# A chunked attention with a rational feed-forward layer on one core: loads sent in pieces behind the streamed sums, plain products in the last two steps

## The chip, the core and the metric

The kernel runs on one core of a Trainium2 chip. The metric is device time in microseconds (us) of one execution. Engines are named as in the profile: PE is TensorE (its weight loads are PEld), DVE is VectorE, ACT is ScalarE, POOL is GpSimd, SP is SyncE, which here only issues DMAs. All numbers are float32; the matmuls take operands split into a high part that TensorE holds exactly and a low rest, and add three products for each (high by high, high by low, low by high).

## What is computed

```
scores = scale * q_c @ k_c.T                  # chunks of 64 tokens, 8 heads of 64, batch 8, 576 tokens
attn = exp(scores - max) / (sum + 1e-9)
x = attn @ v_c                                # 4608 tokens x 512
h = x @ w_in                                  # 512 x 2048
P = a[0] + a[1] * h + a[2] * h**2 + a[3] * h**3
Q = 1.0 + abs(b[0]) * abs(h) + abs(b[1]) * h**2
out = (P / (Q + 1e-6)) @ w_out                # 2048 x 512
```

## The kernel before

**Blocks and steps.** The 4608 tokens are 18 blocks of 256 (`n`, 0 to 17), the 2048 columns of `h` four stages of 512 (`s`). A step `g` is one stage of one block; from block 2 on, g = 4n + s, so there are 72 steps and the last two are 70 and 71. A step is: `ff1`, the product with `w_in` (48 matmuls of 128x256 in two calls, F and Fb, at L347) into the PSUM tile `ph`; a chain of twelve or so elementwise operations on ACT and DVE that ends with `g` at L486 in the tile `C`; and the product with `w_out`. That last product runs two steps behind: on PE the order is F of step g, then the `w_out` product of step g - 2, then F of step g + 1.

**Two forms of the last product.** Up to block 5 it is plain (`ff2`, L423, 48 matmuls of 256 columns, operands `ghi` and `glo`). From block 6 (`FAST`) it is a seven-product scheme that multiplies sums of quarters of `C` by sums of quarters of `w_out` and takes 42 matmuls: `fast_raw` (calls Zr, Zr2; operand `graw`) and `fast_sum` (calls Zs, Zl; operands `shi`, `slo`). The quarters' sums of `C` are made on POOL (L513, L518, L523, L537, and L505 for `graw`). The sums of `w_out` are made once (`sums_of`, on POOL and ACT, tiles `tt` and `hh`, in steps 12 to 21), sent to DRAM, and **streamed** back for each step into four slots of the tile `wo`: `fetch` at L579, 2 MB a step. Slot 0 is fetched when Zr2 of the step before has read it, the low part (h = 1) of slots 1 to 3 after its Zs, the high part (h = 0) after its Zl. So from the end of Zl until Zs of the next step, with F, Zr and Zr2 between, the last 768 KB must land.

**Order of the work.** The order is written out by hand: `START` up to step 11, then `STEADY`, a table of calls for one block that is run for each block in turn; each engine takes its own calls in this order, and so does SP's queue of DMAs. In one block of `STEADY` there are also the parts of the attention of the next blocks: S (scores, PE, 64 matmuls of 64x64), M, U, E, rs, N (softmax on DVE and ACT), T (transposes on PE), K (`at`, a copy on ACT at L303), A (values, PE), X, Y. S comes in the middle of a `w_out` product, after Zr of stage 1; right behind it `next_scores` (L754) issues the loads of the next block's query and key (512 KB each). A comes in the `w_out` product of stage 0; right behind it `load_v` (L130) issues 512 KB of value. `fast_out` adds the seven products up on ACT and DVE (calls P1, o1 to o4; L624 to L636) and issues four DMAs of the output (L640). Making the sums hangs on the call lS, which subtracts `glo` on POOL in the plain steps (L540): after each lS of steps 12 to 21 six pieces of `sums_of` are taken from the list `making`.

**Tiles.** One pool tag, `raw`, has three buffers of 8 KB a partition: during the sums they hold `tt`, `hh` and `qk`, later `graw0`, `graw1` and `qk`. `co` holds the coefficients.

## Time and profile before

| | |
|---|---|
| Median of 3 runs | 937.63 us (936.0 to 939.81) |
| The profiled execution, its own time | 939.04 us |
| Its span, first to last instruction | 937.3 us |
| PE, PEld busy | 93%, 91% |
| DVE, ACT, POOL busy | 80%, 60%, 54% |
| DMA, mean over the span | 176 GB/s |
| Granted TensorE clock, mean | 0.978 of full speed |

The times and rows of the trace come from one profiled execution, whose span leaves out 1.7 us around it. A busy share is a mean over stages; the question for each stage is which engine the others wait for. In the timeline a row's bracket gives the idle time of its engine just before it and what ended it.

### The profile page before, as it was taken

The numbers are of one execution on the slowest core, as the hardware profiler recorded it, in microseconds if no ns is written. First come the engines' busy times: TensorE is split into PE (matmuls) and PEld (weight loads), VectorE is DVE, ScalarE is ACT, GpSimd is POOL, SyncE is SP. The second block draws the span as 40 slices with busy tenths as digits, with TensorE's granted clock in tenths as the row PEclk, the third lists the DMA queues.
The fourth block names the chain that finished last, engine by engine and source line by source line (L and its number), as shares of the span: only waits on it lengthen the run. The fifth ranks groups of instructions, "written<-read, shape, count | busy, mean of one in ns | idle before, by whom it ended". The sixth has DMA issues, their size and how long they took to land.

```text
span 937.3 us, 20950 instructions
## 1 busy us (share of the span) xinstructions
PE 870.3 (93%) x9096; PEld 848.7 (91%) x9096; DVE 749.6 (80%) x673; ACT 562.9 (60%) x602; POOL 506.2 (54%) x318
## 2 busy tenths in 40 slices
PE   2799999989989999998999999999989999999985
PEld 1789999989989999898998999998989999999985
DVE  6899999867767687887778797878878889897771
ACT  4799966464455655555465656556556565666550
POOL 0114210236668635666567666675756767676672
PEclk9799999999999999999999999999999999999997
DMA  7455422102233243767576766667667777666673
GB/s 290 159 181 172 155 80 77 38 21 66 96 135 136 70 165 100 232 212 237 180 247 204 229 212 218 221 208 232 206 195 226 226 222 224 210 210 197 206 232 112
DMA packets 119099, 164.93 MB, mean 176 GB/s; under 512 B 5856, under 2 KB 104160, under 8 KB 115936
## 3 DMA queue, kind: packets, MB, share of 16 engines
q1 hardware_dynamic: 118848, 163.34, 54.4%
q8 instruction: 71, 1.16, 0.5%
q10 hardware_dynamic: 160, 0.26, 0.1%
q14 instruction: 20, 0.16, 0.1%
HBM read 145.76 MB, written 17.83 MB: 175 GB/s over the span
## 4 chain that ended last, share of the span: by engine, by line
PE 72%; DMA 13%; ACT 6%; DVE 5%; POOL 3%; issue 1%; DVEq 0%; SPq 0%; POOLq 0%; ACTq 0%
PE ph L347 34%; PE acc L594 12%; DMA wo<-t 11%; PE acd L594 10%; PE po L423 10%; PE psx L220 2%; DMA raw<-in_w_in 2%; PE pst L299 2%; PE pss L220 2%; ACT at L303 1%; DVE sm L256 1%; POOL glo L540 1%; DMA t<-tt 1%; POOL tt L550 1%; DVE e L262 1%
## 5 line engine op out<-in xcount | busy, mean ns | idle before, releaser
L347 PE MATMUL ph<-xhi,wi_hi 128*128 128x256 f32 x1152 | 326.1, 283 | 10.8 <-ACT at L303 6.4
L347 PE MATMUL ph<-xlo,wi_hi 128*128 128x256 f32 x1152 | 322.5, 280 | 0.1
L347 PE MATMUL ph<-xhi,wi_lo 128*128 128x256 f32 x1152 | 322.3, 280 | 0.0
L347 PEld LDWEIGHTS ph<-xhi,wi_hi 128*128 128x128 f32 x1152 | 217.8, 189 | 16.2 <-ACT at L303 8.6
L347 PEld LDWEIGHTS ph<-xlo,wi_hi 128*128 128x128 f32 x1152 | 217.8, 189 | 0.5 <-DVE xlo L330 0.4
L347 PEld LDWEIGHTS ph<-xhi,wi_lo 128*128 128x128 f32 x1152 | 217.9, 189 | 0.0
L537 POOL TENSOR_TENSOR slo<-B,shi 128x1024 fp32r<-128x1024 f32 x48 | 121.7, 2536 | 85.3 <-ACT shi L529 85.3
L478 DVE SCALAR_TENSOR_TENSOR U<-U,co,ph 128x1024 f32<-128x1024 f32 x60 | 75.7, 1261 | 58.2 <-ACT ph L474 58.2
L457 DVE SCALAR_TENSOR_TENSOR U<-U,co 128x1024 f32<-128x1024 f32 x60 | 98.9, 1649 | 26.4 <-ACT U L448 26.4
L448 ACT ACTIVATE U<-ph 128x1024 f32<-128x1024 f32 x60 | 61.5, 1025 | 91.4 <-PE ph L347 91.4
L505 POOL TENSOR_TENSOR graw<-C,graw 128x768 fp32r<-128x768 f32 x48 | 98.7, 2055 | 31.0 <-ACT graw L500 24.6
L513 POOL TENSOR_TENSOR B<-C 128x512 f32<-128x512 f32 x48 | 75.1, 1564 | 70.7 <-DVE C L486 70.7
L470 ACT ACTIVATE B<-U,cst,co 128x1024 f32<-128x1024 f32 x60 | 74.8, 1246 | 54.7 <-DVE U L457 54.7
L461 DVE TENSOR_TENSOR C<-C,ph 128x1024 f32<-128x1024 f32 x60 | 72.8, 1214 | 33.6 <-ACT U L448 33.6
L423 PE MATMUL po<-wo,ghi 128*128 128x256 f32 (+2 forms) x768 | 93.5, 278 | 0.0
L453 ACT ACTIVATE C<-ph,co 128x1024 f32<-128x1024 f32 x60 | 72.2, 1204 | 31.2 <-PE ph L347 28.0
L423 PEld LDWEIGHTS po<-wo,ghi 128*128 128x128 f32 x768 | 90.6, 188 | 0.0
L594 PE MATMUL acc<-wo,graw 128*128 128x256 f32 x576 | 84.6, 281 | 1.5 <-POOL graw L505 1.5
L474 ACT ACTIVATE ph<-B,co 128x1024 f32<-128x1024 f32 x60 | 67.2, 1120 | 29.1 <-DVE C L465 26.8
L594 PE MATMUL acd<-wo,shi 128*128 128x256 f32 x384 | 64.5, 292 | 21.6 <-DMA wo<-t 19.9
L486 DVE SCALAR_TENSOR_TENSOR C<-C,co,ph 128x1024 f32<-128x1024 f32 x60 | 76.9, 1281 | 2.1
L465 DVE SCALAR_TENSOR_TENSOR C<-C,co,ph 128x1024 f32<-128x1024 f32 x60 | 76.6, 1276 | 1.1
(107 smaller groups left out, 1630.8 us busy)
## 6 DMA issues: line engine op xcount, KB each, us to landing
wo<-t SPq DMA_DIRECT2D x94, 768.0 KB, 6.5
wo<-t SPq DMA_DIRECT2D x102, 256.0 KB, 3.5
v<-in_vP SPq DMA_DIRECT2D x18, 512.0 KB, 4.8
out<-o SPq DMA_DIRECT2D x70, 128.0 KB, 2.6
raw<-in_w_in SPq DMA_DIRECT2D x8, 1024.0 KB, 4.8
raw<-in_w_out SPq DMA_DIRECT2D x8, 1024.0 KB, 4.8
qk<-in_qT SPq DMA_DIRECT2D x16, 512.0 KB, 3.6
qk<-in_kT SPq DMA_DIRECT2D x16, 512.0 KB, 5.0
```

The source lines that it names most:

```text
L347: nc.tensor.matmul(ph[:, fi, :], w[:, cc, f], x[:, cc, :], start=(k == 0), stop=(k == len(mm) - 1))
L423: nc.tensor.matmul(accs[n][i][:, cols], g[:, fi, i * 128:(i + 1) * 128], w[:, FPS * s + fi, cols], start=start, stop=stop,)
L457: nc.vector.scalar_tensor_tensor(U, U, c0, U, ALU.add, ALU.mult)
L461: nc.vector.tensor_mul(C, C, h)
L465: nc.vector.scalar_tensor_tensor(C, C, na1, h, ALU.add, ALU.mult)
L470: nc.scalar.activation(ch[key][2], ch[key][1], AF.Ln, bias=cst[:, 0:1], scale=lsc)
L478: nc.vector.scalar_tensor_tensor(V, V, kq, h, ALU.add, ALU.mult)
L486: nc.vector.scalar_tensor_tensor(C, C, na0, h, ALU.add, ALU.mult)
L505: nc.gpsimd.tensor_sub(lo, quads(ch[steps[g]][3])[:, :, 1:4, :], hi.bitcast(F32))
L513: nc.gpsimd.tensor_sub(S[:, 0:2], q[:, 0:1].to_broadcast([P, 2, 2, 128]), q[:, 1:3])
L537: nc.gpsimd.tensor_sub(lo, sbuf[g], hi.bitcast(F32))
L594: nc.tensor.matmul(acc[n][pair][:, bank, col:col + 256], stat, mov, start=start, stop=stop)
```

## The change

- **Transfers.** Query and key of the next block are no longer sent in two loads behind S but in eight of 256 columns (128 KB each), value in two of 512 columns (256 KB each), and the output's four DMAs are held back too. All go into a list, `later`; after the last fetch of a step (behind Zl) `later_loads` takes two entries from it, 512 KB in all. The output's entries are put ahead of the list.
- **Sums of `w_out`.** The list `making` is cut into groups by `None`: four operations on POOL, four on POOL, then two copies on ACT with four subtractions on POOL and the send. One group is taken at each lS, so that steps 12 to 23 make them, three to each of the four sets.
- **Last two steps.** Steps 70 and 71 take the plain form, 48 matmuls each (`tail_next`, `tail_last`), into a tile `pe` of their own, with `glo` subtracted on DVE and not on POOL. The quarter of `w_out` that the streams have overwritten is saved in DRAM when the sums are sent (`scratch["b", s]`, for stages 2 and 3) and loaded to `b12` (`tail_load`, 2 x 512 KB) at the start of block 17's turn. The seven-product sums of block 17 then end with its stage 1; `fast_out` adds them up behind lS of step 71, and two additions on DVE join them with `pe`.
- **Order.** In `STEADY` PE's own order stays as it was. On ACT E comes behind hR of stage 3, hS of stage 2 behind Ex of stage 3, hR of stage 1 ahead of Ln of stage 2, C of stage 1 ahead of U, and of stage 3 U first, then hR of stage 2, C and Ln; on DVE V of stage 3 goes ahead of M and p of stage 3 behind U; on POOL the parts of the sums of quarters change places, mostly so that `graw` of stage 2 comes before its sums.
- **Tiles.** `graw` starts 96 numbers (384 bytes) into its buffer. `co` is allocated behind the other tiles and not ahead of them, which moves every tile of the pool `p2` down by 128 bytes.

```diff
...
-    "F_0 p2_3-1 lS_2-1 Ln_3-1 Ex_3-1 Fb_0 E+1 lR_2-1 t_3-1 A2_3-1 Zr_2-1 U_0 g_3-1 C_0 Zr2_2-1 V_0 Zs_2-1 hR_3-1 "
+    "F_0 p2_3-1 s4_2-1 Ex_3-1 Fb_0 hS_2-1 t_3-1 lS_2-1 A2_3-1 Zr_2-1 U_0 g_3-1 C_0 Zr2_2-1 V_0 Zs_2-1 hR_3-1 p_0 "
...
-    co = cp.tile([P, 32], F32, tag="co", name="co")
...
+    total = NB * NST
+
     def fast(g):
-        return steps[g][0] >= FAST
+        return NST * FAST <= g < total - 2
...
         if g % 2 not in graw:
-            graw[g % 2] = p2.tile([P, 2, 2, 3, 128], F32R, tag="raw", name=f"graw{g % 2}", bufs=3)
+            t = p2.tile([P, 96 + 1536], F32R, tag="raw", name=f"graw{g % 2}", bufs=3)
+            graw[g % 2] = t[:, 96:].rearrange("p (h j q t) -> p h j q t", h=2, j=2, q=3)
         nc.scalar.copy(graw[g % 2][:, 0], quads(C)[:, :, 1:4, :])
...
-            nc.gpsimd.tensor_sub(lo, C, hi.bitcast(F32))
+            (nc.gpsimd if g < total - 2 else nc.vector).tensor_sub(lo, C, hi.bitcast(F32))
...
         T = [tt[:, i] for i in range(4)]
+        yield None
         yield lambda: whole(T[1], 0, 0)
         yield lambda: whole(T[3], 0, 1)
         yield lambda: nc.gpsimd.tensor_sub(T[1], T[3], T[1])
         yield lambda: whole(T[2], 1, 1)
+        yield None
         yield lambda: nc.gpsimd.tensor_add(T[3], T[2], T[3])
         yield lambda: nc.gpsimd.tensor_add(T[2], T[2], T[1])
         yield lambda: whole(T[0], 1, 0)
         yield lambda: nc.gpsimd.tensor_sub(T[0], T[0], T[2])
+        yield None
...
             nc.sync.dma_start(out=scratch[s][:, 0], in_=hh.bitcast(F32))
             nc.sync.dma_start(out=scratch[s][:, 1], in_=tt)
+            if s >= 2:
+                scratch["b", s] = dr.tile([P, 2, 2, 256], F32, tag=f"b{s}", name=f"b{s}")
+                rows = slice(FPS * s, FPS * s + 3, 2)
+                for h in range(2):
+                    nc.sync.dma_start(out=scratch["b", s][:, h], in_=wo.bitcast(F32)[:, h, rows, 256:512])
...
                         n, s, name, j, stat, h, s == 0 and half == 0 and j == 0 and h == 0 and name == "7",
-                        s == NST - 1 and half == 1 and j == 1,
+                        s == (1 if n == NB - 1 else NST - 1) and half == 1 and j == 1,
                     )
+
+    tail = {}
+
+    def tail_load():
+        b12 = p2.tile([P, 2, 2, 2, 256], F32R, tag="raw", name="b12", bufs=3)
+        tail["b12"] = b12
+        for k in range(2):
+            nc.sync.dma_start(out=b12.bitcast(F32)[:, k], in_=scratch["b", 2 + k])
+
+    def tail_product(g, i, fi, h, stat, start, stop):
+        _, s = steps[g]
+        for c in range(2):
+            if c == 1 and fi % 2 == 0:
+                mov = tail["b12"][:, s - 2, h, fi // 2]
+            else:
+                mov = wo[:, h, FPS * s + fi, 256 * c:256 * c + 256]
+            nc.tensor.matmul(
+                tail["pe"][:, i, 256 * c:256 * c + 256], stat[:, fi, 128 * i:128 * i + 128], mov,
+                start=start and c == 0, stop=stop and c == 1,
+            )
+
+    def tail_next(half):
+        g = total - 2
+        if half == 0:
+            tail["pe"] = bank_pair("p1", "pe")
+        stat = gbuf[steps[g]][half]
+        for fi in range(FPS):
+            for i in range(2):
+                for h in ((0, 1) if half == 0 else (0,)):
+                    tail_product(g, i, fi, h, stat, half == 0 and fi == 0 and h == 0, False)
+
+    def tail_last():
+        g = total - 1
+        hi, lo = gbuf[steps[g]]
+        for i in range(2):
+            mm = [(x, h, fi) for x, h in ((hi, 0), (hi, 1), (lo, 0)) for fi in range(FPS)]
+            for k, (x, h, fi) in enumerate(mm):
+                tail_product(g, i, fi, h, x, False, k == len(mm) - 1)
+            oe = p2.tile([P, DM], F32, tag="AB"[i], name=f"oe{i}")
+            part_ = obuf[NB - 1][:, 2 - 2 * i:4 - 2 * i].rearrange("p a b -> p (a b)")
+            nc.vector.tensor_add(oe, tail["pe"][:, i, :], part_)
+            for u, queue in ((0, nc.sync), (1, nc.scalar)):
+                queue.dma_start(out=rows_out(NB - 1)[i, u], in_=oe[64 * u:64 * u + 64, :])
...
+            if n == NB - 1:
+                return
             for c in range(2):
-                for u in range(UPB):
-                    half = o[64 * u:64 * u + 64, 2 - 2 * c:4 - 2 * c].rearrange("p a b -> p (a b)")
-                    (nc.scalar if n == NB - 1 and u else nc.sync).dma_start(out=rows_out(n)[c, u], in_=half)
+                def send(c=c):
+                    for u in range(UPB):
+                        half = o[64 * u:64 * u + 64, 2 - 2 * c:4 - 2 * c].rearrange("p a b -> p (a b)")
+                        nc.sync.dma_start(out=rows_out(n)[c, u], in_=half)
+
+                later.insert(c, send)
...
+    co = p2.tile([P, 32], F32, tag="co", name="co", bufs=1)
+    na0, na1, na2, na3, c0, kq, lsc, ebias, ib, b1m, nib = (co[:, i:i + 1] for i in range(11))
     newton_coefficients()
     tt = p2.tile([P, 4, 512], F32, tag="raw", name="tt", bufs=3)
     hh = p2.tile([P, 4, 512], F32R, tag="raw", name="hh", bufs=3)
     qk = p2.tile([P, 2, W], F32, tag="raw", name="qk", bufs=3)
...
-    making = [f for s in range(NST) for f in sums_of(s, tt, hh)]
+    making = [f for s in range(NST) for f in sums_of(s, tt, hh)][1:]
...
-                nc.sync.dma_start(out=qk[:, i, :], in_=src[n + 1])
+            for c in range(4):
+                def send(c=c):
+                    cols = slice(256 * c, 256 * c + 256)
+                    for i, src in enumerate((qT, kT)):
+                        nc.sync.dma_start(out=qk[:, i, cols], in_=src[n + 1][:, cols])
+
+                later.append(send)
...
-        load_v(n + 1)
+        if n + 1 < NB:
+            v = loaded["v", n + 1] = p2.tile([P, W], F32, tag="vt", name=f"v{n + 1}", bufs=1)
+            for c in range(2):
+                cols = slice(512 * c, 512 * c + 512)
+                later.append(lambda cols=cols: nc.sync.dma_start(out=v[:, cols], in_=vP[n + 1][:, cols]))
...
         elif op in chain:
             chain[op](g)
             if op == "lS":
-                for _ in range(6):
-                    if making:
-                        making.pop(0)()
+                while making:
+                    f = making.pop(0)
+                    if f is None:
+                        break
+                    f()
+                if g == total - 1:
+                    for k in range(5):
+                        fast_out(NB - 1, k)
+        elif g == total - 2:
+            if op in ("Zr", "Zl"):
+                tail_next(int(op == "Zl"))
+        elif g == total - 1:
+            if op == "Zl":
+                tail_last()
         elif not fast(g):
             if op == "Zr":
...
+                later_loads()
         elif op in ("Zr", "Zr2"):
             fast_raw(g, op == "Zr2")
-            if op == "Zr2" and g + 1 < total:
+            if op == "Zr2" and fast(g + 1):
                 for h in range(2):
                     fetch((s + 1) % NST, slice(0, 1), h)
         else:
             fast_sum(g, op == "Zl")
-            if g + 1 < total:
+            if fast(g + 1):
                 fetch((s + 1) % NST, slice(1, 4), 1 if op == "Zs" else 0)
+            if op == "Zl":
+                later_loads()
+
+    def later_loads():
+        for f in later[:2]:
+            f()
+        del later[:2]
 
     items = [re.fullmatch(r"(\w+?)(?:_(\d))?([+-]\d+)?", item).groups() for item in STEADY.split()]
     for b in range(FIRST // NST, NB + 1):
+        if b == NB - 1:
+            tail_load()
...
-                if n >= FAST:
+                if NB - 1 > n >= FAST:
                     fast_out(n, ("P1", "o1", "o2", "o3", "o4").index(op))
-                elif op == "P1" and n not in made["O"]:
+                elif op == "P1" and n < FAST and n not in made["O"]:
```

On SP's queue, in one block of the steady part (`t1` to `t3` and `t0` are the streamed sums of the four stages; 128x2x256 is slot 0, 128x6x256 slots 1 to 3; x2 is one for each part; `o` is the output, `v` value, `qk` query and key), there stood before:

```order
L640 DMA out_0<-o9_6278 64x512 x4
L579 DMA wo_71<-t1_2883 128x2x256 x2
L130 DMA v12_6407<-in_vP 128x1024
L579 DMA wo_71<-t1_2883 128x6x256 x2
L754 DMA qk_2003<-in_qT 128x1024
L754 DMA qk_2003<-in_kT 128x1024
L579 DMA wo_71<-t2_3179 128x2x256 x2
L579 DMA wo_71<-t2_3179 128x6x256 x2
L579 DMA wo_71<-t3_3631 128x2x256 x2
L579 DMA wo_71<-t3_3631 128x6x256 x2
```

and now:

```order
L588 DMA wo_71<-t1_3045 128x6x256 x2
L697 DMA out_0<-o9_6332 64x512 x4
L588 DMA wo_71<-t2_3471 128x2x256 x2
L588 DMA wo_71<-t2_3471 128x6x256 x2
L828 DMA v12_6458<-in_vP 128x512 x2
L588 DMA wo_71<-t3_3931 128x2x256 x2
L588 DMA wo_71<-t3_3931 128x6x256 x2
L818 DMA qk_2003<-in_qT 128x256
L818 DMA qk_2003<-in_kT 128x256
```

The loads of value and of query and key, and the output's DMAs, have moved from ahead of a step's fetches to behind the last one of them; of the four pairs of query and key pieces two go behind this step's fetches and two behind the next's.

On POOL, steps 13 to 16 (`glo` is lS, with its step's number; the rows of `tt` are pieces of `sums_of`), there stood before:

```order
L540 TENSOR_TENSOR glo13_2454<-C13_2200,ghi13_2399 128x1024
L550 TENSOR_TENSOR tt_2001<-wo_71 128x512
L560 TENSOR_TENSOR tt_2001<-tt_2001 128x512
L563 TENSOR_TENSOR tt_2001<-tt_2001,hh_2002 128x512 x2
L540 TENSOR_TENSOR glo14_2584<-C14_2338,ghi14_2535 128x1024
L563 TENSOR_TENSOR tt_2001<-tt_2001,hh_2002 128x512 x2
L550 TENSOR_TENSOR tt_2001<-wo_71 128x512 x2
L555 TENSOR_TENSOR tt_2001<-tt_2001 128x512
L550 TENSOR_TENSOR tt_2001<-wo_71 128x512
L540 TENSOR_TENSOR glo15_2741<-C15_2495,ghi15_2663 128x1024
```

and now:

```order
L541 TENSOR_TENSOR glo14_2611<-C14_2336,ghi14_2494 128x1024
L567 TENSOR_TENSOR tt_2001<-tt_2001,hh_2002 128x512 x4
L541 TENSOR_TENSOR glo15_2744<-C15_2530,ghi15_2661 128x1024
L551 TENSOR_TENSOR tt_2001<-wo_71 128x512 x2
L557 TENSOR_TENSOR tt_2001<-tt_2001 128x512
L551 TENSOR_TENSOR tt_2001<-wo_71 128x512
L541 TENSOR_TENSOR glo16_2878<-C16_2658,ghi16_2787 128x1024
```

The first operations of the second set, which write `tt` again, stood right behind the four subtractions after which `tt` is sent; now `glo15` and a step's time lie between, and no `glo` waits behind more than four operations.

On DVE, at the end of the program (`U71` and `C71` are tiles of step 71's chain, `o17` the output of block 17), there stood before:

```order
L478 SCALAR_TENSOR_TENSOR U71_10439<-U71_10439,co_76,ph17_3_10366 128x1024
L482 SCALAR_TENSOR_TENSOR ph17_3_10366<-U71_10439,ph17_3_10366 128x1024
L486 SCALAR_TENSOR_TENSOR C71_10437<-C71_10437,co_76,ph17_3_10366 128x1024
L630 TENSOR_TENSOR o17_10590<-acc17_10305,o17_10590 128x2x256
L632 TENSOR_TENSOR o17_10590<-acd17_10306,o17_10590 128x2x256
L634 TENSOR_TENSOR o17_10590<-acd17_10306,o17_10590 128x512
L636 TENSOR_TENSOR o17_10590<-acc17_10305,o17_10590 128x256
```

and now:

```order
L478 SCALAR_TENSOR_TENSOR U71_10531<-U71_10531,co_1991,ph17_3_10461 128x1024
L541 TENSOR_TENSOR glo70_10574<-C70_10412,ghi70_10533 128x1024
L482 SCALAR_TENSOR_TENSOR ph17_3_10461<-U71_10531,ph17_3_10461 128x1024
L486 SCALAR_TENSOR_TENSOR C71_10536<-C71_10536,co_1991,ph17_3_10461 128x1024
L541 TENSOR_TENSOR glo71_10629<-C71_10536,ghi71_10611 128x1024
L684 TENSOR_TENSOR o17_10631<-acc17_10395,o17_10631 128x2x256
L686 TENSOR_TENSOR o17_10631<-acd17_10396,o17_10631 128x2x256
L688 TENSOR_TENSOR o17_10631<-acd17_10396,o17_10631 128x512
L690 TENSOR_TENSOR o17_10631<-acc17_10395,o17_10631 128x256
L668 TENSOR_TENSOR oe0_10661<-pe_10577,o17_10631 128x512
L668 TENSOR_TENSOR oe1_10689<-pe_10577,o17_10631 128x512
```

The additions of block 17 have moved behind `glo71` and no longer wait for the product of step 71, the subtraction `glo70` has come into step 71's chain, and two additions (`oe0`, `oe1`) are last.

## Rows read from the trace of the kernel before

**Rows 1.** The profile's page: the busy time of each engine (share of the span, number of instructions).

```profile
PE 870.3 (93%) x9096; PEld 848.7 (91%) x9096; DVE 749.6 (80%) x673; ACT 562.9 (60%) x602; POOL 506.2 (54%) x318
```

**Rows 2.** The waits, longest first in total, for PE over the whole span: who waited for whom, us in total, times, longest us.

```profile
PE acd L594 <- DMA wo<-t: 20.5, 12, 3.7
...
PE ph L347 <- ACT at L303: 6.4, 11, 4.7
```

**Rows 3.** The timeline of PE, from the first seven-product block on: first matmuls of F of some steps (`ph<-xhi,wi_hi`), and a wait in front of Zs (`acd<-wo,shi`). Columns: start us, us, engine, line, operation, out<-in, count, and in brackets the idle time before it and what ended it.

```profile
361.65 0.29 PE L347 MATMUL ph<-xhi,wi_hi 128*128 128x256 f32 x1
...
761.61 0.28 PE L347 MATMUL ph<-xhi,wi_hi 128*128 128x256 f32 x1
...
773.49 0.36 PE L347 MATMUL ph<-xhi,wi_hi 128*128 128x256 f32 x1
...
782.60 0.70 PE L594 MATMUL acd<-wo,shi 128*128 128x256 f32 x4 [1.10 <-DMA wo<-t]
...
831.19 0.28 PE L347 MATMUL ph<-xhi,wi_hi 128*128 128x256 f32 x1
...
842.73 0.39 PE L347 MATMUL ph<-xhi,wi_hi 128*128 128x256 f32 x1 [0.18 <-ACT at L303]
...
854.73 0.28 PE L347 MATMUL ph<-xhi,wi_hi 128*128 128x256 f32 x1
...
865.34 0.28 PE L347 MATMUL ph<-xhi,wi_hi 128*128 128x256 f32 x1
```

**Rows 4.** The chain of work that ended last, in order of time (start us, us, what): the 48 matmuls of F in two steps, and two waits for a fetch, counted from the end of Zl before it.

```profile
773.36 9.11 DMA wo<-t
...
808.79 9.15 DMA wo<-t
...
821.06 5.44 PE ph L347 x48
...
865.50 5.66 PE ph L347 x48
```

**Rows 5.** Busy time of each engine in some stretches (us from the span's start; the last three columns are the granted clock, the mean busy share of the 16 DMA engines, and GB/s).

```profile
686.00:690.00 4.00, 3.55 (x20) 3.58 (x21) 3.90 (x6) 2.15 (x2) 3.92 (x4) 0.67 0.34 98
...
812.00:814.00 2.00, 2.00 (x20) 2.00 (x19) 1.93 (x3) 0.74 (x1) 1.18 (x1) 1.00 1.07 379
...
816.00:818.00 2.00, 1.84 (x70) 1.57 (x62) 1.26 (x2) 1.37 (x2) 1.84 (x3) 1.00 0.05 11
...
820.00:830.00 10.00, 10.00 (x90) 10.00 (x89) 8.59 (x7) 6.30 (x6) 5.18 (x3) 1.00 0.63 196
...
914.00:918.00 4.00, 3.62 (x17) 3.65 (x18) 0.10 (x1) 0.83 (x1) 3.68 (x3) 0.50 0.41 128
```

**Rows 6.** The timeline of SP's queue: issues of query, key and value, and the fetches behind the first two (columns as in rows 3; the us of a merged row run from its first issue to its last).

```profile
769.99 0.35 SPq L754 DMA_DIRECT2D qk<-in_qT  x1
770.39 0.42 SPq L754 DMA_DIRECT2D qk<-in_kT  x1
770.92 26.01 SPq L579 DMA_DIRECT2D wo<-t  x12
...
806.13 0.34 SPq L130 DMA_DIRECT2D v<-in_vP  x1
```

**Rows 7.** The timeline of POOL, ACT and PE, columns as in rows 3, while the sums of `w_out` are made.

```profile
242.03 2.59 POOL L550 TENSOR_TENSOR tt<-wo 128x512 f32<-128x512 f32 x2 [6.92 <-DMA t<-tt]
...
247.22 2.40 POOL L540 TENSOR_TENSOR glo<-C,ghi 128x1024 fp32r<-128x1024 f32 x1
...
255.90 1.05 ACT L571 CAST hh<-tt 128x1024 fp32r<-128x1024 f32 x1 [2.96 <-POOL tt L560]
...
260.87 0.58 PE L347 MATMUL ph<-xhi,wi_hi 128*128 128x256 f32 x1 [4.66 <-ACT at L303]
```

**Rows 8.** The chain of work that ended last, F of that step and of the next.

```profile
260.87 7.36 PE ph L347 x48
...
275.39 5.92 PE ph L347 x48
```

**Rows 9.** The timeline of PE and DVE at the end, columns as in rows 3.

```profile
907.77 1.10 PE L594 MATMUL acc<-wo,graw 128*128 128x256 f32 x8
...
914.38 1.20 PE L594 MATMUL acd<-wo,shi 128*128 128x256 f32 x4 [1.63 <-DMA wo<-t]
...
925.51 0.71 PE L594 MATMUL acd<-wo,shi 128*128 128x256 f32 x4 [3.65 <-DMA wo<-t]
...
910.24 1.28 DVE L478 SCALAR_TENSOR_TENSOR U<-U,co,ph 128x1024 f32<-128x1024 f32 x1 [1.34 <-ACT ph L474]
...
912.81 1.28 DVE L486 SCALAR_TENSOR_TENSOR C<-C,co,ph 128x1024 f32<-128x1024 f32 x1
...
932.60 0.41 DVE L636 TENSOR_TENSOR o<-acc,o 128x256 f32<-128x256 f32 x1
```

**Rows 10.** The chain of work that ended last: four matmuls of the product of step 70.

```profile
916.43 0.85 PE acd L594 x4
```

**Rows 11.** Groups of instructions by form over the whole span: busy us, mean ns of one, idle time before them.

```profile
L397 DVE TENSOR_TENSOR glo<-B,A 128x1024 fp32r<-128x1024 f32 x8 | 9.8, 1220 | 0.1
...
L496 ACT CAST ghi<-C 128x1024 fp32r<-128x1024 f32 x12 | 12.5, 1044 | 2.9 <-DVE C L486 2.9
...
L632 DVE TENSOR_TENSOR o<-acd,o 128x512 f32<-128x512 f32 x12 | 8.3, 691 | 0.4
```

More of the change, by code (lines that the diff above doesn't have):

```diff
@@ L99, in tile_chunked_attention_rational_moe @@
     WS = 256.0
-    na0, na1, na2, na3, c0, kq, lsc, ebias, ib, b1m, nib = (co[:, i:i + 1] for i in range(11))
     TINY = 2.0 ** -60
@@ L616, in fast_sum @@
                         n, s, name, j, stat, h, s == 0 and half == 0 and j == 0 and h == 0 and name == "7",
-                        s == NST - 1 and half == 1 and j == 1,
+                        s == (1 if n == NB - 1 else NST - 1) and half == 1 and j == 1,
                     )
+    tail = {}
[36 more added lines that the diff above has]
+                queue.dma_start(out=rows_out(NB - 1)[i, u], in_=oe[64 * u:64 * u + 64, :])
+    later = []
     def fast_out(n, k):
@@ L727, in tile_chunked_attention_rational_moe @@
     run(START, "F")
-    total = len(steps)
+    co = p2.tile([P, 32], F32, tag="co", name="co", bufs=1)
+    na0, na1, na2, na3, c0, kq, lsc, ebias, ib, b1m, nib = (co[:, i:i + 1] for i in range(11))
     newton_coefficients()
```

10 rows, old and new, of the table STEADY are left out of this document.

## Prediction

> **What bounds the kernel now.** I read the busy times first: PE is busy for 93% of the span, the next engine, DVE, for 80% [rows 1]. PE is the bound, so the question is where PE stands still or runs slowly. The waits of PE answer it: from the middle of the program on, one reason returns, the fetch of the streamed sums (`wo<-t`), 20.5 us in 12 waits [rows 2]. The timeline shows where: in front of Zs, once a block, as the 1.10 us at 782.60 [rows 3]. SP's queue shows why it is that step and no other: 12 us earlier, behind S, query and key (2 x 512 KB) were issued at 769.99 and 770.39, and the fetches only behind them [rows 6]. The last fetch of that step then took 9.11 us from the end of Zl [rows 4]. In the step before, 512 KB of value stand ahead of the fetches [rows 6], the last of which also took 9.15 us [rows 4]; there S, 64 matmuls on PE, lies in the time given. The reader is to see that the DMAs are not full: 512 KB, or the 2 MB of a step, move at up to 379 GB/s, and a few us later almost nothing moves, share 0.05 [rows 5]. What is late is an order, not a bandwidth.
>
> A wait costs more than its idle time and gives something back. After a long one the granted clock falls: 0.67 in 686 to 690 and 0.50, the 1.2 GHz level, in 914 to 918 [rows 5]. On the other hand F's 48 matmuls take 5.44 us in some steps, mostly those behind such a wait, and 5.66 us where PE has run without a stop, both at full clock [rows 4]. I don't know why; I use both as prices.
>
> Two other places stand out. While the sums of `w_out` are made, PE waits 4.66 us at 260.87 for a copy on ACT [rows 7]. Back along the rows: ACT stood behind `hh`, `hh` waited for POOL, and POOL had waited 6.92 us until `tt` had been sent before it could write it again, with `glo` behind [rows 7]. F right after this takes 7.36 us, where the next one takes 5.92 [rows 8]. And at the end PE waits for fetches that have no F in front to hide them (1.63 and 3.65 us), at the low clock in between [rows 9, 5].
>
> **The change part by part.**
>
> *Transfers.* Removed: everything that stands ahead of a step's fetches. To find what a block then takes I add up four steps without a wait for a fetch, F to F [rows 3]: with T, 831.19 to 842.73, 11.54 us; with A, 842.73 to 854.73, 12.00; with S, 761.61 to 773.49, 11.88; with none, 854.73 to 865.34, 10.61. The first ran at the fast pace; F and the product are 90 matmuls, and at the slow pace they take 90 x (5.66 - 5.44) / 48 = 0.41 us more [rows 4]. Sum 46.44 us. Ten blocks are 464.4 us; they took 842.73 - 361.65 = 481.1 us [rows 3]. Gain **16.7 us**. That is about the 15 us of fetch waits that lie there (20.5 less the two at the end), plus the low clock, less the fast pace.
>
> What the pieces may cost: after the last fetch, 512 KB follow. A step's 2 MB keep the DMAs busy for 6.3 us (0.63 of 10 us) [rows 5], so 512 KB take 1.6 us, and the next fetch is issued more than 7 us later, behind F and Zr. I cost them at nothing; the hiding work is F. If they are not done by then, each step waits up to 1.6 us, or 1.1 us if there is slack of 0.5 us (9.11 less the wait of 1.10 are 8.0 us given; with 512 KB less ahead the 9.15 us would be 7.5). SP's issues, 0.35 to 0.42 us each [rows 6], fall into the same gap.
>
> The Trainium skill speaks against pieces: SBUF — State Buffer, section "The DMA setup-cost knee", gives each transfer some 2 us that don't depend on its size and advises the largest single transfer. By it the four pieces behind a step would be an estimated 4 x 2 = 8 us where the sum here has 1.6, and the forecast would become the third rival. The row in which several transfers together fill the DMA engines (share 1.07) [rows 5] says that such times overlap.
>
> *Sums of `w_out`.* Now a step lies between the send of `tt` and its next writing, longer than the 6.92 us. Removed: 4.66 us and 7.36 - 5.92 = 1.44 us, **6.1 us**. Next late there is POOL itself: `glo` 2.40 us and four operations of 1.3 us (2.59 for two) [rows 7] are under 8 us of a step of 12. The saves of `w_out` and the later sends (the last set is now finished in step 23) could hold up slot 3 for step 24: from nothing to 3.7 us, the longest wait for a stream [rows 2]. I take nothing, since Zs of step 24 comes a whole F and Zr later. The same bounds and choice for the 1 MB of `b12`.
>
> *Last two steps.* The product of step 70 begins at 907.77 [rows 9]. Matmuls at 5.66 / 48 = 0.118 us [rows 4]. High part, 32: until 911.6. `glo70` on DVE stands behind the operation that ends at 910.24 + 1.28 = 911.5 [rows 9] and takes 1.22 us, by the operation of the same form at L397 [rows 11]: 912.7, so the 16 low ones end at 914.6. Step 71's chain ended at 912.81 + 1.28 = 914.1 [rows 9]; with `glo70` in it, 915.3; `ghi71` 1.04 us [rows 11], 916.4; `glo71` at 917.6 is in time. Then 24 matmuls until 919.2 and 24 until 922.0, an addition of 0.69 us [rows 11], 922.8 with a little for the handover. Before, 4.3 us lay from the end of the last addition (932.60 + 0.41) to the end of the span [rows 9]. New end 927.1 for 937.3: 10.2 us less. The two gaps of PE (1.1 and 1.8 us) may bring the low clock back: at 0.85 us for four [rows 10] 24 matmuls cost 2.3 us more. I take half, so **9.1 us**. The twelve matmuls more are in this.
>
> *Order and tiles.* PE's order is the same; elsewhere operations change places within a step. In the steps added up above no engine but PE was the last, so I take nothing; bounds 1 us a block either way (the size of the wait at 782.60). That a tile's place changes an operation's time is shown by no row; nothing, with the two paces of F as bounds.
>
> Sum: 16.7 + 6.1 + 9.1 = 31.9 us. The span 937.3 becomes 905.4, the profiled execution's own 939.04 becomes 907.1, and, since that execution was 1.4 us over the median, the median 937.63 becomes **905.7 us**.
>
> **The rivals.**
> 1. *The fast pace holds.* If F and the product run at 5.44 us' pace throughout, each of the 40 steps of the ten blocks gains 0.41 us more: 16.4 us, 889.3. For it: moved tiles, two paces at the same clock. Against: five steps at the end, with no waits, all at the slow one (the 5.66 us is of these).
> 2. *A new wait in the place of the old.* With PE at 46.4 us a block, DVE, ACT or POOL may now be last once a block, through the new order. At 1 us a block, 915.7. For it: DVE's 80%, and the small wait for L303 that stays [rows 2, 3]. Against: 820 to 830 has PE at 10.00 of 10.00 with DVE at 8.59 [rows 5].
> 3. *The pieces stand in the next step's way.* The 512 KB behind a step delay the next one's fetches. At 1.1 to 1.6 us in each of 40 steps, 44 to 64 us are lost: 950 to 970, slower than before. It decides from 31.9 / 40 = 0.8 us a step on. For it: up to 2.5 MB in a step of 10.6 to 12 us. Against: the empty DMAs at 816 [rows 5].
> 4. *The waits don't come from these loads* and the transfers change nothing: 937.6 - 15.2 = 922.4. Against: the queue's order [rows 6].
>
> **How the numbers follow.** Forecast, 895 to 913: 0.65. First rival 0.10, second 0.13, third 0.04, fourth 0.05, something else 0.03. The range reaches to the second rival and half of the first: 893 to 920, which leaves out half of the first, the third, the fourth and the rest, 0.17. About 0.5% is what a measurement of this kernel can tell from no change. Faster by more: 0.93 (forecast and rivals 1, 2, 4); slower: 0.04; the same: 0.03.
>
> **What would show it.** PE's waits for `wo<-t` fall from 20.5 us to under 3; the distance of F's in steps without attention is 10.6 us, and ten blocks take 464 us. There is no wait of POOL for `t<-tt`, and no gap of PE above 1 us between 250 and 265. At the end PE has two gaps, for `glo70` and `ghi71`, and some 5 us lie between its last matmul and the end of the span. It is wrong if Zs still waits for `wo`, if steps are shorter than 10.3 us (first rival), or if a new name leads PE's waits with 8 us or more.

## The result and the profile after

| | before | after |
|---|---|---|
| Median | 936.82 us (931.53 to 939.81, 4 runs) | 899.12 us (897.37 to 901.35, 4 runs) |
| Ratio, with its 95% interval | | 0.9605 [0.9556, 0.9654] |
| Profiled execution: own time, span, clock | 939.04, 937.3 us, 0.978 | 899.64, 897.4 us, 0.994 |

After is faster by 37.7 us; forecast were 31.9. The span, 39.9 us shorter (the profiled execution of before lay 2.2 us over its median), falls into three pieces. They are cut at the start of the F of step 26, the last one ahead of the first seven-product step, and of the F of step 66, ten blocks later. PE's timeline of after, rows that answer to [rows 3] (columns as there):

```profile
356.68 0.30 PE L345 MATMUL ph<-xhi,wi_hi 128*128 128x256 f32 x1
...
813.81 0.38 PE L345 MATMUL ph<-xhi,wi_hi 128*128 128x256 f32 x1 [0.17 <-ACT at L301]
...
825.52 0.28 PE L345 MATMUL ph<-xhi,wi_hi 128*128 128x256 f32 x1
...
835.74 0.28 PE L345 MATMUL ph<-xhi,wi_hi 128*128 128x256 f32 x1
...
846.34 0.28 PE L345 MATMUL ph<-xhi,wi_hi 128*128 128x256 f32 x1
...
856.56 0.28 PE L345 MATMUL ph<-xhi,wi_hi 128*128 128x256 f32 x1
```

| stretch | before | after | saved | forecast |
|---|---|---|---|---|
| up to 356.68 (361.65 before) | 361.65 | 356.68 | 5.0 | 6.1 |
| ten blocks, to 813.81 (842.73) | 481.08 | 457.13 | **23.95** | 16.7 |
| from there to the end | 94.6 | 83.6 | 11.0 | 9.1 |

The waits of PE in after, against [rows 2] (who for whom, us in total, times, longest us): the fetch has gone from 20.5 us to 0.7, K from 6.4 to 1.6, and the last steps have three small new ones.

```profile
PE ph L345 <- ACT at L301: 1.6, 10, 0.2
PE pe L644 <- ACT ghi L496: 1.5, 1, 1.5
PE pe L644 <- DVE oe L668: 1.2, 1, 1.2
...
PE pe L644 <- DVE glo L541: 0.9, 1, 0.9
...
PE acd L603 <- DMA wo<-t: 0.7, 2, 0.4
```

The chain of waits of after shows what the forecast had not counted on. In the last steps, with no attention between, F takes 5.46 and 5.66 us by turns, where the forecast had seen only the slow time [rows 4]. The starts above say the same: 10.22 us from 825.52 on, then 10.60, then 10.22.

```profile
846.50 5.46 PE ph L345 x48
...
856.72 5.66 PE ph L345 x48
...
867.33 5.47 PE ph L345 x48
```

The stretch that stood in [rows 5] as full on PE, and the end of the span (columns as there): the clock is full in both.

```profile
820.00:830.00 10.00, 10.00 (x142) 9.81 (x142) 8.33 (x7) 6.67 (x7) 7.11 (x5) 1.00 0.57 173
877.00:893.00 16.00, 12.43 (x101) 11.78 (x99) 10.45 (x12) 2.45 (x4) 0.00 (x0) 1.00 0.06 16
```

### The profile page after: what moved, and what is told of

Same layout as the page of the kernel before. It is cut to its first block, busy times and chain, and to the rows that moved or that the text cites. A ratio compares the mean times of both kernels' runs of the same rounds, so it can differ in the third digit from the quotient of the medians.

```text
span 897.4 us, 21094 instructions
## 1 busy us (share of the span) xinstructions
PE 856.5 (95%) x9108; PEld 835.9 (93%) x9108; DVE 763.7 (85%) x677; ACT 556.1 (62%) x600; POOL 478.9 (53%) x308
## 4 chain that ended last, share of the span: by engine, by line
PE 80%; DVE 7%; DMA 5%; ACT 5%; issue 1%; SPq 0%; DVEq 0%; ACTq 0%
PE ph L345 41%; PE acc L603 13%; PE po L421 11%; PE acd L603 10%; DMA raw<-in_w_in 3%; DMA wo<-t 2%; PE psx L218 2%; PE pss L218 2%; PE pst L297 1%; ACT at L301 1%; DVE sm L254 1%; DVE ghi L382 1%; DVE e L260 1%; DVE B L390 1%; DVE xlo L328 1%
## 5 line engine op out<-in xcount | busy, mean ns | idle before, releaser
L538 POOL TENSOR_TENSOR slo<-B,shi 128x1024 fp32r<-128x1024 f32 x46 | 110.5, 2403 | 70.6 <-ACT shi L530 70.6
L506 POOL TENSOR_TENSOR graw<-C,graw 128x768 fp32r<-128x768 f32 x46 | 93.2, 2026 | 38.2 <-ACT graw L501 38.0
L457 DVE SCALAR_TENSOR_TENSOR U<-U,co 128x1024 f32<-128x1024 f32 x60 | 91.7, 1528 | 23.2 <-ACT U L448 23.2
L514 POOL TENSOR_TENSOR B<-C 128x512 f32<-128x512 f32 x46 | 80.0, 1740 | 54.8 <-DVE C L486 54.8
L421 PE MATMUL po<-wo,ghi 128*128 128x256 f32 (+2 forms) x768 | 94.6, 279 | 1.7 <-DVE ghi L382 1.7
L603 PE MATMUL acc<-wo,graw 128*128 128x256 f32 x552 | 79.4, 279 | 0.0
L482 DVE SCALAR_TENSOR_TENSOR ph<-U,ph 128x1024 f32<-128x1024 f32 x60 | 73.4, 1224 | 1.2
```

The lines of the kernel that those rows point to most:

```text
L421: nc.tensor.matmul(accs[n][i][:, cols], g[:, fi, i * 128:(i + 1) * 128], w[:, FPS * s + fi, cols], start=start, stop=stop,)
L457: nc.vector.scalar_tensor_tensor(U, U, c0, U, ALU.add, ALU.mult)
L482: nc.vector.scalar_tensor_tensor(h, V, 2.0, h, ALU.subtract, ALU.mult)
L506: nc.gpsimd.tensor_sub(lo, quads(ch[steps[g]][3])[:, :, 1:4, :], hi.bitcast(F32))
L514: nc.gpsimd.tensor_sub(S[:, 0:2], q[:, 0:1].to_broadcast([P, 2, 2, 128]), q[:, 1:3])
L538: nc.gpsimd.tensor_sub(lo, sbuf[g], hi.bitcast(F32))
```

## The experiments

Each is an edit of after, unless it says before. "Ten blocks" is the stretch of the table above. Ratios are to runs of before on the same chip; their intervals are some 0.2 to 0.5% to either side, so two kernels that differ by less are compared by the stretches of their traces. F's mean pace is taken over the 40 F of the ten blocks, start to start within an F: 0.1172 us a matmul before, 0.1152 after. This mean has two parts, as the single matmuls of the traces show. Behind its first few matmuls every one of these F runs at one of two steady paces, 113.3 or 117.8 ns, and the first interval of an F can be longer, up to some 220 ns behind a wait. An F is called fast when its last 24 matmuls are 113.3 ns apart: 13 of the 40 before, 30 after.

**The two tiles put back.**

```diff
+    co = cp.tile([P, 32], F32, tag="co", name="co")
...
-            t = p2.tile([P, 96 + 1536], F32R, tag="raw", name=f"graw{g % 2}", bufs=3)
-            graw[g % 2] = t[:, 96:].rearrange("p (h j q t) -> p h j q t", h=2, j=2, q=3)
+            graw[g % 2] = p2.tile([P, 2, 2, 3, 128], F32R, tag="raw", name=f"graw{g % 2}", bufs=3)
...
-    co = p2.tile([P, 32], F32, tag="co", name="co", bufs=1)
...
```

> The kernel after with its two moved tiles put back: co among the constants again, so that every rotating tile lies 128 bytes higher, and graw at the start of its slot. Theory A (the place of the tiles that PE reads sets the faster of its two paces, 0.1136 against 0.118 us a matmul): F returns to 5.6 us in most steps, ten blocks (F of step 26 to F of step 66) take 464 us instead of 457.1, the time is 906 to 909 us. Theory B (the order of the instructions and the missing waits set the pace): ten blocks stay at 457 us and the time at 898 to 901 us.

904.15 us, 0.9632 [0.9608, 0.9656]; ten blocks 461.28, 4.15 us more than after, with waits for `wo<-t` of 2.5 us in all, 1.8 more than after. F's mean pace is 0.1159, and 22 of 40 are fast. The two ratios don't separate this kernel from after, since their intervals overlap; the next run does show that the places do something. But theory A as it stands falls: in the last steps of this kernel, with the tiles where before had them, F ran at the fast time, as its chain of waits shows.

```profile
849.20 5.44 PE ph L347 x48
...
859.50 5.44 PE ph L347 x48
```

**Before, with the two tiles moved and nothing else** (the same lines the other way round).

> The kernel before with nothing changed but the place of the two tiles (co behind the rotating tiles, graw 384 bytes into its slot). Theory A (places set the pace): F runs at 0.1136 us a matmul also in steps without a wait ahead; the waits for wo<-t stay at some 20 us, and the time falls by 4 to 8 us, to 929 to 933 us. Theory B (order and waits set it): the same as before, 935 to 938 us.

933.77 us, 0.995 [0.993, 0.9969]: faster by 0.5%, some 5 us, with an interval that does not reach 1. Waits for `wo<-t` 21.0 us, ten blocks 478.14, 2.94 us less than before, and 24 of 40 F fast for 13. The time lies between the ranges, 0.8 us over theory A's and 1.2 under theory B's.

**Loads and output sent at once again.**

```diff
...
-            for c in range(4):
-                def send(c=c):
...
-                later.append(send)
+                nc.sync.dma_start(out=qk[:, i, :], in_=src[n + 1])
...
+        load_v(n + 1)
```

> The kernel after with query, key, value and output sent whole and at once where their step stands, as before; all else as after. The forecast's term for the transfers is 16.7 us: 914 to 918 us if the faster pace is not their doing (theory A), 921 to 925 us if the end of the waits also brought the pace (theory B, 24 us for ten blocks). Both expect waits for wo<-t of 15 to 20 us. If the waits do not come from these loads, 899 us.

919.26 us, 0.9788 [0.9764, 0.9812]; ten blocks 482.98. The waits of PE, in us in total, times and longest, are back:

```profile
PE acd L603 <- DMA wo<-t: 15.2, 7, 3.0
...
PE acd L603 <- ACT e L267: 3.8, 2, 1.9
```

The time lies between the two expectations, 1.3 us over theory A's and 1.7 under theory B's. F's mean pace here is 0.1157 us a matmul, close to after's 0.1152, so the end of the waits is not what made F faster. The ten blocks are 25.9 us longer than in after, and 17.7 of these are waits of PE (20.5 for 2.8); among them are two for ACT that neither before nor after has. The granted clock is 0.99 in this stretch, for 1.00 in after; what else is in the other 8 us was not found. Which of the loads (query and key, value, output) costs how much was not run.

**Before, with the transfers alone moved** (`later`, `later_loads` and the pieces as in the diff, the rest as before).

> The kernel before with the transfers alone sent as in after (pieces of 256 KB behind the streamed sums); order, sums of w_out, tail and tiles as before. Theory A (places set the pace): the waits for wo<-t fall to the two at the end, the pace stays at 0.118 us a matmul, ten blocks take 464 us and the whole 919 to 922 us. Theory B (the missing waits set the pace): ten blocks take 457 us, the whole 911 to 914 us.

919.96 us, 0.98 [0.9775, 0.9825]; ten blocks 462.83. The waits for `wo<-t` fall to 5.2 us, most of them at the end of the program:

```profile
PE acd L594 <- DMA wo<-t: 5.2, 6, 3.6
```

F stays at 0.1170 a matmul, with 16 of 40 fast for 13 before. Theory B is out: with the waits gone and the tiles where they were, the slow pace stays. The transfers' term alone is 481.08 - 462.83 = 18.25 us; the medians on this chip differ by 18.9 (938.88 to 919.96).

**The old order.** The table `STEADY` of before in the kernel after:

```diff
-    "F_0 p2_3-1 s4_2-1 Ex_3-1 Fb_0 hS_2-1 t_3-1 lS_2-1 A2_3-1 Zr_2-1 U_0 g_3-1 C_0 Zr2_2-1 V_0 Zs_2-1 hR_3-1 p_0 "
+    "F_0 p2_3-1 lS_2-1 Ln_3-1 Ex_3-1 Fb_0 E+1 lR_2-1 t_3-1 A2_3-1 Zr_2-1 U_0 g_3-1 C_0 Zr2_2-1 V_0 Zs_2-1 hR_3-1 "
...
```

> The kernel after with the order of the kernel before in the steady part (only the table of the order is undone). The forecast costed the order at nothing: 898 to 901 us, ten blocks 457 us, the waits of PE as in after. Rival: the new order keeps DVE and ACT from being late once a block; then waits of about 1 us a block come back, ten blocks take 460 us or more, and the time is 903 to 909 us. A third possibility is that the order alone changes which of its paces PE falls into: no new waits, but F's mean pace is no longer 0.1152 us a matmul.

898.74 us, 0.9563 [0.9528, 0.9599]: the order is worth nothing that can be measured. Ten blocks are 460.84, 3.7 us more, with 2.5 us of waits for `wo<-t`, F at 0.1162 and 25 of 40 fast; the whole does not show it.

**The old grouping of the sums.**

```diff
...
-                while making:
-                    f = making.pop(0)
-                    if f is None:
-                        break
-                    f()
+                for _ in range(6):
+                    if making:
+                        making.pop(0)()
```

> The kernel after with the sums of w_out made six operations a step again. The forecast's term: 6.1 us, so 904 to 906 us, with POOL's wait of some 7 us for t<-tt and PE's wait of 4.7 us behind it back. Rival: the gain of the first stage came from the order or the tiles; then 899 us and the wait stays away.

903.72 us, 0.9619 [0.9581, 0.9657], 4.7 to 5.0 us over the two kernels on the same chip whose sums are new (898.74, 899.0). POOL's wait and PE's are back, as in [rows 7]; first a row of POOL's timeline, then one of PE's:

```profile
237.92 3.55 POOL L551 TENSOR_TENSOR tt<-wo 128x512 f32<-128x512 f32 x2 [7.12 <-DMA t<-tt]
```

```profile
257.68 0.39 PE L345 MATMUL ph<-xhi,wi_hi 128*128 128x256 f32 x1 [3.43 <-ACT at L301]
```

**The old last two steps** (seven products there, `tail_next` and `tail_last` gone).

```diff
...
-        return NST * FAST <= g < total - 2
+        return g >= NST * FAST
...
```

> The kernel after with the last two steps by the seven products again. The forecast's term: 9.1 us (10.2 if the clock is not low in the gaps), so 908 to 910 us. Rival: the waits for wo<-t at the end came from the loads ahead of them and are gone with the transfers moved; then the plain products save next to nothing, and the time is 899 to 903 us.

906.43 us, 0.965 [0.9612, 0.9687], 7.4 to 7.7 us over the same two; in the trace (of an execution 2.3 us over the median) 95.0 us from the F of step 66 to the end, against 83.6. The rival falls by two rows of PE's timeline in this kernel: the waits at the end do not come from loads ahead of the fetches.

```profile
882.56 1.19 PE L603 MATMUL acd<-wo,shi 128*128 128x256 f32 x4 [4.80 <-DMA wo<-t]
...
893.85 0.71 PE L603 MATMUL acd<-wo,shi 128*128 128x256 f32 x4 [3.77 <-DMA wo<-t]
```

**Held back, but whole.**

```diff
-            for c in range(4):
...
+            for i, src in enumerate((qT, kT)):
+                later.append(lambda i=i, src=src: nc.sync.dma_start(out=qk[:, i, :], in_=src[n + 1]))
```

> The kernel after with query and key as one transfer of 512 KB each and value as one of 512 KB, still held back behind the streamed sums (query and key both behind one step, so 1 MB there). If what counts is only that they stand behind the fetches and not that they are in pieces: 899 us, no waits for wo<-t above 1 us. By the row of 6.3 us for 2 MB, 1 MB behind a step takes 3 to 4 us, less than the 7 us to the next fetch. Rival: 1 MB reaches into the next step's fetches; then a wait of 1 to 2 us in each of 12 blocks comes back, 910 to 920 us.

899.0 us, 0.9582 [0.9542, 0.9622], with 2.8 us of waits for `wo<-t` in 5, the longest 1.4 us; ten blocks 459.67. What pays is the place behind the fetches, not the pieces. The Trainium skill's advice of the largest single transfer (SBUF — State Buffer, "The DMA setup-cost knee"), given there for DMA-bound transfers, is neither borne out nor refuted by these two times: with 0.7 and 2.8 us of waits, both kernels hide the transfers.

**F alone, the moving tile at eight places.** 48 matmuls of F between short other work; nothing else is computed. The moving tile is the operand that streams through TensorE, here `x`; the weights are the operand that is loaded first, here `w_in`. Distance means the place of the moving tile less that of the weights, in bytes of 256.

```diff
...
+    for off in range(0, 128, 16):
+        idle()
+        product(off)
+        for cut in (256, 280, 304, 336):
+            pair(cut)
+            product(off)
+        small()
+        product(off)
...
```

> A kernel of F alone: the 48 matmuls of one step's first product, repeated, with the moving tile at eight places (residues 128, 192, 256, 320, 384, 448, 0, 64 bytes of 512; the kernel before has 192, after has 64), and at each place six times: behind an idle gap, behind a pair of matmuls of 256 + 256 columns, of 280 + 232, of 304 + 208, of 336 + 176, and behind 16 matmuls of a quarter. Everything else of the computation is left out. Theory A (the place sets the pace): the pace differs from place to place and not with what stands ahead, about 0.1136 at 64 and 0.118 to 0.120 at 192. Theory B (what stands ahead sets it, whatever the place): at every place the same two or three paces, 0.1134, 0.118 and 0.120, one for each predecessor. Theory C: both, the place sets which paces there are and the predecessor chooses among them. Rival: neither; then F runs at one pace in all 48 cases, and the two paces of the kernels come from the other engines' reads.

The chain of waits shows each F as one row. Here the weights lie at 128 of 512 bytes; the first three rows have the moving tile at 128 (behind the gap), at 192 and at 256; the last three at 320, behind the gap, behind 256 + 256 and behind 280 + 232.

```profile
47.17 5.76 PE ph L105 x48
...
85.08 5.66 PE ph L105 x48
...
122.41 5.70 PE ph L105 x48
...
160.03 5.46 PE ph L105 x48
...
165.72 5.65 PE ph L105 x48
...
171.61 5.45 PE ph L105 x48
```

The places 384, 448, 0 and 64 repeat these four to 0.02 us: what counts is the place within 256 bytes. Theory C holds in this kernel: at a distance of 0 F has one time, 5.76 us, behind the first four predecessors; 64 bytes below the weights (192 of 256) there are two, 5.46 and 5.65, and the predecessor goes with them. Here, with no other engine reading for F, these are the very times of the kernels. Behind the last two predecessors F is longer at every place, mostly by its first interval (some 150 and 220 ns).

**F alone, weights and moving tile both moved** (four places of the one by eight of the other, each behind 280 + 232 and 256 + 256).

```diff
...
+    for at in range(0, 64, 16):
+        for off in range(0, 64, 8):
+            for cut in (280, 256):
+                pair(cut)
+                product(off, at)
...
```

> F alone again, with the weights at four places (0, 64, 128, 192 bytes of 256) and the moving tile at eight (every 32 bytes of 256), each behind a pair of matmuls of 280 + 232 columns and behind one of 256 + 256; everything else of the computation is left out. In the run before this one the weights lay at 128 and the moving tile was fast at 64 and 320 (0.1136, and 0.1177 behind 256 + 256), slow at the rest. Theory D (the distance of the two counts): the fast place moves with the weights, 192 for weights at 0, 0 for 64, 64 for 128, 128 for 192. Theory E (the place of the moving tile alone): it stays at 64. If a place is at 0.1136 behind both pairs, it would take away the slow half of the steps. Rival: the place alone does nothing without the strides of the real weights; then all 64 cases agree.

Start to start of F's matmuls in ns (first to last, over 47), behind 280 + 232 / 256 + 256, by distance of the moving tile from the weights, in bytes of 256:

```
distance       0           64          128         192
weights 0    120 / 120   118 / 118   119 / 120   114 / 118
        64   120 / 120   114 / 118   119 / 120   113 / 118
       128   120 / 120   118 / 118   119 / 119   114 / 114
       192   120 / 120   114 / 113   120 / 119   118 / 118
```

Theory D, in part: 0 is slow and 128 nearly so wherever the weights lie, and only 64 and 192 reach 113 to 114. But the same distance is fast in one row and slow in another; which of the two paces, the distance does not settle. Nor does the pair ahead: with the weights at 128 and a distance of 192, F ran at 118 behind 256 + 256 in the kernel before this one and at 114 here. The odd places (32, 96, ...) gave 117 to 120. As the programs place their tiles (`w_in` at 128 of 256 bytes, `x` at 192 before and at 64 after), before has the distance 64 between `x` and `w_in`, after 192: both of the good kind.

**Distance zero in the kernel.**

```diff
+    shift = p2.tile([P, 16], F32, tag="shift", name="shift", bufs=1)
+    nc.gpsimd.memset(shift, 0.0)
```

> The kernel after with 64 bytes more in front of the rotating tiles, so that x, g and graw lie at the same place of 256 bytes as the weights they meet (distance 0, where F alone ran at 0.1200 us a matmul in every case; after has a distance of 64 bytes, with 0.1136 and 0.118). Nothing else changes. Theory C (the place sets the paces, what stands ahead chooses): every F at 0.1200; 90 matmuls a step at 0.1200 instead of F's mean of 0.1152 are 0.43 us a step, 17 us in ten blocks (474 us), 25 us in the 59 steps from step 13 on: 920 to 926 us. Rival (the pace is set by order, waits and the other engines; places matter only by chance): 897 to 902 us.

920.54 us, 0.9792 [0.9761, 0.9824]; ten blocks 471.61, F's mean pace 0.1204. All 40 F run at 120.0 ns, none at 113.3 or 117.8. The rival is out: 64 bytes more in front of the tiles cost some 20 us. They move the operands of the other engines too, but in the chain of waits of this kernel F takes the time that F alone took at this distance:

```profile
843.83 5.76 PE ph L348 x48
854.63 5.76 PE ph L348 x48
865.43 5.76 PE ph L348 x48
```

**The last matmul ahead of F split.**

```diff
...
+                        cut=152 if half == 1 and name == "3" and j == 1 else 256,
```

> The kernel after with the last matmul in front of F (the second of Zl's last product) made as two, of 152 and 104 columns, so that F is not entered behind an unbroken row of 256 columns; in F alone this kept the pace of 0.1136 where 256 + 256 gave 0.118. It costs one matmul more a step, at most 0.05 us, or 3 us in all. Theory C: F runs at 0.1136 to 0.1145 in the steps without attention, no longer every other one at 0.1177; ten blocks 450 to 455 us, the whole 892 to 897 us, faster than after. Rival: what stands ahead is not decided by the last matmul alone; then the paces change places but keep their mean, and the time is 899 to 902 us.

900.03 us, 0.9591 [0.9553, 0.963]: no gain. F takes 5.52 us and 5.71 in steps without a wait, for 5.46 and 5.66 in after, but its steady paces have not changed: 113.3 and 117.8 ns, with 29 of 40 fast for 30. What grew is the first interval of F, to some 180 ns where after has 115 to 124; hence the mean of 0.1163, and ten blocks of 458.49. PE's timeline shows it, the first three matmuls of an F here:

```profile
844.56 0.34 PE L345 MATMUL ph<-xhi,wi_hi 128*128 128x256 f32 x1
844.74 0.28 PE L345 MATMUL ph<-xlo,wi_hi 128*128 128x256 f32 x1
844.85 0.28 PE L345 MATMUL ph<-xhi,wi_lo 128*128 128x256 f32 x1
```

and of the same F in after:

```profile
846.34 0.28 PE L345 MATMUL ph<-xhi,wi_hi 128*128 128x256 f32 x1
846.47 0.28 PE L345 MATMUL ph<-xlo,wi_hi 128*128 128x256 f32 x1
846.58 0.28 PE L345 MATMUL ph<-xhi,wi_lo 128*128 128x256 f32 x1
```

Theory C's range is missed, and the time is the rival's. The cut of 152 + 104 is none of those that ran in F alone, so the run tells only that this cut does not choose the pace. No version here beats after by more than the measurement is uncertain.

## Why the prediction was right, and where it was off

**Transfers.** The mechanism is shown from both sides: moved alone they save 18.25 us in ten blocks, sent at once they cost 25.9. The term of 16.7 was 1.6 us small, which is less than like kernels differ by (455.8 to 460.8 us, below). The third rival (pieces in the next step's way) and the fourth (waits from elsewhere) did not happen. Nor did the second: in the ten blocks of after PE waits 2.8 us in all.

**The step that was mis-sized** is the pace and, with it, "order and tiles: nothing". Ten blocks were summed with F at 5.66 us, and the forecast took nothing for a tile's place, since no row showed it to matter. It does. The 23.95 us are, from kernel to kernel: 481.08 to 462.83 by the transfers (18.25), to 461.28 by order, sums and tail (1.55), to 457.13 by the two tiles (4.15, of which 1.8 are waits for `wo<-t`; 2.94 when moved in before). So the first rival happened in part: ten blocks are 7.3 us under the forecast's 464.4, of its 16.4, with F at 5.46 in many steps and still at 5.66 in others. Eight steps of after without attention took 10.21 to 10.22 us, under the 10.3 that the prediction gave as the sign of this rival. The argument against that rival, five slow steps at the end without a wait, held for before and not as a rule: the same steps run at 5.44 in one kernel and by turns in another.

The size of the tiles' share stays rough, since kernels with the same places and almost no waits took from 455.8 (old sums) to 460.8 us (old order) for the ten blocks. The count of fast F tells the same: 13 of 40 before, 16 with the transfers alone, 24 with the tiles alone, 22 with all but the tiles; 25 with all but the order; 26 to 34 in the six kernels that have after's order and tiles. So the tiles raise it, but they are not the whole cause, and the share of the order is not told from the spread of like kernels.

By another cut of the 23.95 us, PE's waits in the ten blocks fell from 17.9 us to 2.8, and 8.9 us are left; 17 more fast steps at the prediction's 0.41 us are an estimated 7.0 of them, if the products go at the pace of their F.

**Sums of `w_out`.** From the F of step 14 (206.23 before, 208.25 after) to the end of that stretch 7.0 us were saved; undone, 4.7 came back in the trace. The forecast's 6.1 lies between. PE has no gap above 1 us between 250 and 265, as foreseen; POOL still waits for `t<-tt`, but at 250.07 for 2.50 us and not 6.92, and PE has no gap behind it. The 2 us lost ahead of step 14 can be put down to no edit: in the kernels with the same start that F begins between 203.78 and 208.25.

**Last two steps.** 10.2 us by the sum, 9.1 with half of a low clock; measured 11.0, undone 11.4 in the trace, but 7.4 to 7.7 in the whole time. The clock did not fall, so the half was wrong. PE's timeline has the two gaps foreseen, and a third that the sum lacks: the second half's matmuls waited until DVE had read the first half of the same tile `pe`.

```profile
882.23 0.38 PE L644 MATMUL pe<-wo,glo 128*128 128x256 f32 x1 [0.94 <-DVE glo L541]
...
885.84 0.38 PE L644 MATMUL pe<-wo,ghi 128*128 128x256 f32 x1 [1.48 <-ACT ghi L496]
...
890.08 0.39 PE L644 MATMUL pe<-wo,ghi 128*128 128x256 f32 x1 [1.16 <-DVE oe L668]
```

## What to carry to other kernels

When a stream has a deadline, send everything that has none behind it, in pieces or whole; read the lateness in the order of the queue, not in the mean bandwidth. When back-to-back matmuls show two or three fixed paces at the same clock, look at where the moving tile lies against the weights before looking for a wait: a shift of 64 bytes cost 20 us here, as much as the largest edit saved. Read the pace from the single matmuls and not from the time of the whole group, which a late second matmul makes longer at the same pace. And when a kernel has two paces, give the forecast both and a middle, not the one that the last steps happened to show.

## What was not expected of the hardware

At full clock (1.00 in the ten blocks of after and in F alone) a matmul of 128x256 took from 113 to 120 ns start to start. In the kernels with distances of 64 and 192 bytes each F settled at 113.3 or 117.8 ns and kept to it; with equal places it was 120 in every F. The distance of the two operands within 256 bytes sets which paces there are. No F of any run had a mean under 113. The Trainium skill (TensorE: Matmul & The Clock Gate, "Back-to-back issue gap") gives N / 2.4 + 2.5 for an isolated one, an estimated 109 ns for 256 columns, and says that in a stream the weight loads set the spacing too. The rows lie 4 to 11 ns above the first; what part of this the weight loads have, no run here shows. Why 64 and 192 bytes have two paces, and what in the work ahead picks one, stays open: the same pair of matmuls ahead went with both, and splitting one matmul left them as they were.
